# Attention and a gated unit in one fp32 kernel: a low part placed behind two maxima, the tails of the matmul units paired elsewhere, and the output weights split one round sooner

## The chip, the cores and the metric

The kernel runs on one core of a Trainium2 chip. The metric is the device time of the program in microseconds, as the median of several runs; lower is better. TensorE (PE) does the matmuls and its weight loads are listed apart (PEld); VectorE is DVE, ScalarE is ACT, GpSimd is POOL, and SyncE (SP) only issues transfers.

## The reference

`x` is 2048 x 448. One branch is a multi-head attention (16 heads of 28), the other a gated unit with 1792 hidden features; a gate computed from `x` mixes them.

```python
qkv = (x @ wqkv) -> q, k, v per head
scores = einsum("bhqd,bhkd->bhqk", q, k) * (Dh ** -0.5)
p = softmax(scores)
a = (p @ v, heads side by side) @ wo
gate = x @ W_gate
up = x @ W_up
gate = gate * (gate > 0)
b = (gate * up) @ W_down
g = sigmoid((x * gate_w).sum(-1, keepdims=True))
out = g * a + (1 - g) * b
```

## The kernel before

**Arithmetic.** Most matmuls run on float32 operands that are split into a rounded high part and a low part, the remainder. The high part is a cast (`act_high` on ACT, `dve_high` on DVE); the low part is a subtraction (`low` on DVE, `pool_low` on POOL). A product is then the sum of high x high, low x high and high x low. The contraction has 448 rows, three chunks of 128 and one of 64, and the 64 rows' high and low parts share one chunk, so one result tile of 128 x 512 takes `NT` = 11 passes (`TERMS`). Such a result is called a unit here. The last pass of a unit, its tail, needs 64 rows only.

**Order.** The order on every engine is the program's order, written out by hand; a tile pool only decides which buffer a tile gets and so what it has to wait for. PSUM has three tags: `s` with two tiles of 128 x 512, `mx` with two tiles of twice that size (`ps_w`), and `x` with two tiles of 128 x 512.

**First stage.** `qk` and `vproj` compute the projections, with matmuls for the first row maxima mixed in. `qk` ends with a cast on ACT, a `low` on DVE and a transfer from POOL's queue to `qk_d`. Before all that, `WARM` matmuls on zeros run on PE while the first inputs load. The last projection unit, `qk(0, 6)`, keeps its result in the second half of a tile named `pair`; the first half of that tile holds the raw weights of the first gate/up unit. `pair` sits in a buffer of the tag `Q`, and `load_q(2)` takes that tag's next buffer that comes free.

**Rounds.** The attention then runs in rounds (line 569). Each has an order string, read letter by letter: `s` is a score matmul of 128 x 512 with its exponential on ACT, `m` a maximum (two matmuls into a `ps_w` tile, one reduction on DVE), `x` one pass of a gate/up unit, `u` the split of the second half of the first gate/up weights with loads, `h` the paired tails. In a pair, the tail of one unit uses rows 0 to 63 of the array and that of the other rows 64 to 127; `SECOND` says which unit has the upper rows. At a round's end the weights of the next units are split (`split_f`) and `pv` multiplies the round's probabilities with V, 64 matmuls into a tile `po` that is copied to (ACT) or added to (DVE) the tile `os`.

There are 32 rounds: one `FIRST`, 28 `LONG` or `WIDE` ones, and three `LATE` ones, in which no maxima are left. A `LATE` round takes two score matmuls at a time into one `ps_w` tile, with one exponential over 128 x 1024 (`scores_pair`); its four gate/up units use the tag `s`, its `po` the tag `x`, and its relu and the casts of the weights run on DVE. The gate/up passes of the first unit follow `HIGH_FIRST`: six passes with the high weights, then those with the low ones.

**Last stage.** Five gate/up units of two results each (`gate_up`) are interleaved with the down projection (`down_mm`, 12 matmuls into `acc` each), then come the output projection (`wout`, with the weights `WO`) and more of the down projection. `split_wo` makes `WO` from the raw `wor` with two casts on ACT and two subtractions on POOL.

Lines that the steps touch: `WARM` line 34, `FIRST` 43, `LATE` 48, the end of `qk` 305 to 308, `SECOND` 430, `pv` 488, the loop over the rounds 569 to 630, `gate_up` 666.

Of the kernel before, what the change touches and what calls it, by code (L numbers as in the profile page):

```python
# [18 lines left out]
P = 128  # L19
# [7 lines left out]
NF = F // P  # L27
NB = 4
TB = 512
NK = S // P  # L30
SCALE = DH ** -0.5
VC = D + 2
NQ = 2 * D // P
WARM = 9

EARLY = (5, 5, 4, 4, 4, 3, 3, 3, 2, 2, 2, 2, 1, 1, 1, 1)

# [2 lines left out]

FIRST = "s" * 12 + "mmssmxxsxxusxmxsxsmxsmxsxsmxsxsmxsxsmxsxsxmsxsxmsxsxmsx"

LONG = "mxsmsxxxxxsmsxsmsxxsmsxsmsxxsmxxsmsxsxxsmsxxsxsmxsxsmsxxsmsxsmsxxsmsxsxxsmsmxssh"
WIDE = "sxxmxmxxsxxmsxxsxsmxxssxmxmxsxxsxxsxsmsxxsmxssxxxsmsxxsxmsxmsxsxmsxsmxsxsxxsmsxxsmsmsxxsxsh"

LATE = "ssxxxssxxxssxxxssxx" * 2 + "ssxxxssxxxssxxssxx" * 2 + "h"

ROUNDS = [(FIRST, 2)] + ([(LONG, 3)] * 2 + [(WIDE, 4)]) * 2 + [(LONG, 3)] * 2  # L50

# [6 lines left out]
NT = len(TERMS)  # L58
# [9 lines left out]
def gated_mix_kernel(ctx, tc, x, wq, wo, wgu, wd, out):  # L68
    nc = tc.nc
# [7 lines left out]
    def f32(ap):  # L77
        return ap.bitcast(F32)
# [4 lines left out]
    def ps_w(name):  # L83
        return psum.tile([P, 2, TB], F32, tag="mx", bufs=2, name=name)

    def ps_x(name):
        return psum.tile([P, TB], F32, tag="x", bufs=2, name=name)
# [7 lines left out]
    def low(dst, src, high):  # L95
        nc.vector.tensor_tensor(dst, src, f32(high), op=OP.subtract)  # L96
# [5 lines left out]
    qk_d = dram.tile([2, 2 * D, S], F32, name="qk_d")  # L102
# [92 lines left out]
    def xf(tb, b):  # L195
        return X[tb][b // 4][:, b % 4]

    WR, WS, HK, pair = {}, {}, {}, []

    def fetch_f(i):  # L200

# [8 lines left out]
    with tc.tile_pool(name="qkv", bufs=1) as pa:  # L210
# [89 lines left out]
        def qk(tb, c, terms=TERMS, among=()):  # L300
            ps = ps_any(f"qk_{tb}_{c}", c == NQ - 1)
            for n, (a, b) in enumerate(terms):
                nc.tensor.matmul(ps, W[:, a, c * P:(c + 1) * P], xf(tb, b), start=(n == 0), stop=(n == NT - 1))  # L303
                mix(n, among)
            st = st_tile(tb, c)
            act_high(st[:, 0], ps)
            low(st[:, 1], ps, st[:, 0])
            nc.gpsimd.dma_start(qk_d[:, c * P:(c + 1) * P, tb * TB:(tb + 1) * TB].rearrange("r d t -> d r t"), f32(st))

        def vproj(tb, t, among=()):  # L310
            ps = ps_any(f"v_{tb}_{t}", tb == 0 and t > 1)
# [26 lines left out]
        ps = ps_x("warm_ps")  # L338
        for n in range(WARM):
            nc.tensor.matmul(ps, warm[:, :P], warm, start=True, stop=True)  # L340
# [38 lines left out]
        units = [(qk, 3, 1), (qk, 2, 2), (qk, 3, 2)]  # L379
# [3 lines left out]
        units = units[2:]  # L383
        while units or vs:
            mixed += units[:1] + vs[:1]
            units, vs = units[1:], vs[1:]
        spills = {15 + 3 * k: (NB - 1 - k // 2, k % 2) for k in range(6)}
        m, first, ahead = 0, 9, 2 * LEAD + 4
        for n, (f, *a) in enumerate(mixed):
# [15 lines left out]
            among, ends = [], m  # L405
# [21 lines left out]
    att = stk.enter_context(tc.tile_pool(name="att", bufs=1))  # L427

    done = sum(n for _, n in ROUNDS) // 2
    SECOND = {sum(n for _, n in ROUNDS[:r + 1]) - 1 for r in range(len(ROUNDS)) if "h" in ROUNDS[r][0]}  # L430
    SECOND |= set(range(2 * done + 1, 2 * NB * NF, 2))

    def lane(k):
        return slice(64 * k, 64 * k + 64)
# [1 line left out]
    def split_f(i, high, low, part=(0, 1)):  # L436

        if part[0] == 0:
            WS[i] = fe.tile([P, 2, 7, P], F32R, name=f"wg_{i}", tag="wg", bufs=2)
        w, wr = WS[i], WR[i]  # L440
        for s in part:
            high(w[:, s, 0:3], wr[:, s, 0:3])
            low(w[:, s, 3:6], wr[:, s, 0:3], w[:, s, 0:3])
        if part[-1] == 1:
            high(w[:, :, 6], wr[:, :, 3])
            for s in range(2):
                rows = lane(1 - (2 * i + s in SECOND))
                low(w[rows, s, 6], wr[rows, s, 3], w[rows, s, 6])
            del WR[i]
# [4 lines left out]
    def gu_mm(ps, i, s, n):  # L454

        a, b = (BY_CHUNK if i else HIGH_FIRST)[n]
        rows = slice(0, P)
        if n == NT - 1 and 2 * i + s in SECOND | {k - 1 for k in SECOND}:
            rows = lane(int(2 * i + s in SECOND))
        nc.tensor.matmul(ps, WS[i][rows, s, a], xf(i // NF, b)[rows], start=(n == 0), stop=(n == NT - 1))  # L460
        c = b % 4
        if i % NF == NF - 1 and s and i < NB * NF - 1 and (n == NT - 1 or BY_CHUNK[n + 1][1] % 4 != c):
            for r in range(2):
                nc.sync.dma_start(f32(X[0][r])[:, c], x_d[i // NF + 1, r][:, c])
# [3 lines left out]
    def relu(i, ps, late=False):  # L468
        RL[i] = fe.tile([P, TB], F32, name=f"rl_{i}", tag="rl", bufs=2)
        if late:  # L470
            nc.vector.tensor_scalar_max(RL[i], ps, 0.0)
        else:
            nc.scalar.activation(RL[i], ps, AF.Relu)
# [4 lines left out]
    def spill_h(i, ps):  # L478
        h = fe.tile([P, TB], F32, name=f"h_{i}", tag="h", bufs=2)
        hidden(i, ps, h)  # L480
        h_d[i] = dram.tile([P, TB], F32, name=f"h_d_{i}")
        nc.gpsimd.dma_start(h_d[i], h)  # L482


    NI = H * NK
    OS, LS = {}, {}

    def pv(i0, ni, late):

        h = i0 // NK  # L490
        po = ps_x(f"po_{i0}") if late else ps_w(f"po_{i0}")[:, 0]
        for i in range(i0, i0 + ni):
            p = PT.pop(i)
            for j in range(NB):
                nc.tensor.matmul(po[32 * j:32 * j + 32], V[:, h // 4 % 2, i % NK, h % 4], p[:, j], start=(i == i0),  # L495
                                 stop=(i == i0 + ni - 1))
        if i0 % NK == 0:
            OS[h] = fe.tile([P, TB], F32, name=f"os_{h}", tag="os", bufs=2)
            nc.scalar.activation(OS[h], po, AF.Copy)
        else:  # L500
            nc.vector.tensor_tensor(OS[h], po, OS[h], op=OP.add)  # L501
        if (i0 + ni) % NK == 0:
            LS[h] = fe.tile([P, 16], F32, name=f"ls_{h}", tag="ls", bufs=2)
            nc.gpsimd.dma_start(LS[h], OS[h][DH::32].rearrange("j (p c) -> j p c", c=16))
# [39 lines left out]
    nxt = parts = i0 = 0  # L544
# [24 lines left out]
    for r, (order, nu) in enumerate(ROUNDS):  # L569
        ni = order.count("s") // NB  # L570
        late = order == LATE
        todo = list(range(nxt, nxt + nu))
        nxt += nu
        small_things(i0 // 4)
        if m % (2 * NK) == 0 and i0 <= NI - LEAD:
            smax_end(m // (2 * NK) - 1)
        if late and wor is None:
            wor = load_wo()

        passes = [(*divmod(k, 2), n) for k in todo for n in range(NT - ("h" in order and k >= nxt - 2))]  # L580
        units = []
        ns = 0
        for o in order:
            if o == "x" and not passes:
                continue
            if o == "s":
                i, j = i0 + 1 + ns // NB, ns % NB
                if ns == 4 * NB:
                    small_things(i0 // 4 + 1)
                if len(EARLY) <= i * NB + j < NI * NB and not late:  # L590
                    scores(i, j)
                elif late and i < NI and j % 2 == 0:
                    scores_pair(i, j)
                ns += 1
            elif o == "m":
                smax(m)
                m += 1
            elif o == "x":
                i, half, n = passes.pop(0)
                if n == 0:  # L600
                    ps = (ps_s if late else ps_x)(f"gu_{i}_{half}")
                    units.append((i, half, ps))
                gu_mm(units[-1][2], i, half, n)
                if n == NT - 1:
                    i, half, ps = units.pop()
                    spill_h(i, ps) if half else relu(i, ps, late)
            elif o == "u":
                split_f(0, act_high, pool_low, (1,))
                load_k(2)
                load_q(2)  # L610
                fetch_f(2)
                parts = 2
            elif o == "h":
                for i, half, ps in units:
                    gu_mm(ps, i, half, NT - 1)
                for i, half, ps in units:
                    spill_h(i, ps) if half else relu(i, ps, late)
        assert not passes, (r, passes)

        ready = nxt + (ROUNDS[r + 1][1] if r + 1 < len(ROUNDS) else 2)  # L620
        ready += ready % 2
        while parts < ready:
            split_f(parts // 2, dve_high if late else act_high, pool_low, (parts % 2,))
            parts += 1
            if parts % 2 == 0:
                fetch_f(parts // 2 + 1)
        pv(i0, ni, late)
        i0 += ni
        if late and i0 == NI:
            split_wo(wor)  # L630
    assert i0 == NI and m == len(maxima), (i0, m)
    stk.close()
# [33 lines left out]
    def gate_up(i):  # L666
        if i + 1 < NB * NF:
            split_f(i + 1, act_high, low)
        if i + 3 < NB * NF:
            fetch_f(i + 3)  # L670
        ps = ps_w(f"gu_{i}")
        for s in range(2):
            for n in range(NT - 1):
                gu_mm(ps[:, s], i, s, n)
        for s in range(2):
            gu_mm(ps[:, s], i, s, NT - 1)
        relu(i, ps[:, 0])
        spill_h(i, ps[:, 1])

# [51 lines left out]
    todo = [(gate_up, done), (row_sums, H - 1), (gate_up, done + 1)]  # L731
# [12 lines left out]
    for tb, load, split, at in ((0, 2, (3, 4), (5, 6, 7, 8)), (1, 5, (7, 9), (10, 11, 14, 14)), (2, 21, (23, 25), (28,) * 4),  # L744
                                (3, 35, (37, 39), (42,) * 4)):
        before(load, (fetch_o, tb))
        for k, i in enumerate(split):
            n = todo.index((down, i))
# [53 lines left out]
```

## Time and profile before

| | us |
|---|---|
| median of 3 runs | 1298.44 (1298.35, 1298.44, 1300.04) |
| the profiled execution, its time | 1299.74 |
| its span, first to last instruction | 1297.6 |
| outside the span | 2.14 |
| PE busy | 1290.2 |
| DVE busy | 817.3 |
| ACT busy | 763.0 |
| POOL busy | 367.3 |

The first `LATE` round begins at about 1018 us of the span, the last stage at 1092.3 us. A row of a timeline gives the start, how long the group lasted, the engine, the line, the operation, the tiles it writes and reads, the number of instructions merged, and in brackets the idle time before them with what ended it. Matmuls are pipelined: the time from one start to the next is the cost of a pass, and the duration shown for one is longer than that.

### The profile page before, as it was taken

How to read it: one execution, taken by the hardware profiler on the slowest of the kernel's cores; microseconds unless marked ns; L12 is line 12 of the kernel's file. 1: busy time of each engine (PE TensorE's matmuls, PEld its weight loads, DVE VectorE, ACT ScalarE, POOL GpSimd, SP SyncE). 2: the span in 40 equal slices, each digit the busy share in tenths (PEclk: the TensorE clock that was granted, in tenths of full speed). 3: DMA queues.
4: the chain of work that ended last, by engine and by line, in shares of the span. 5: the costliest groups of instructions: out<-in, count | busy, mean ns of one | idle time of the engine just before them, and what ended most of it. 6: DMA issues, size and time to landing. Idle time of an engine off the chain costs nothing.

```text
span 1297.6 us, 17707 instructions
## 1 busy us (share of the span) xinstructions
PE 1290.2 (99%) x6685; PEld 901.8 (69%) x6685; DVE 817.3 (63%) x849; ACT 763.0 (59%) x1387; POOL 367.3 (28%) x551
## 2 busy tenths in 40 slices
PE   9999999999999999999999999999999999999998
PEld 6888766666666666666666666666666656899997
DVE  6487766667677676777666667767677333663342
ACT  5212776666767777777776666767676755322121
POOL 3222122332313222222223322313132354641020
PEclk9999999999999999999999999999999999999999
DMA  9845523151427223141535142422341222744432
GB/s 311 293 159 230 154 75 98 57 122 47 118 66 192 73 78 99 54 100 47 135 104 121 57 104 69 110 68 82 78 135 35 92 82 88 247 136 151 135 109 77
DMA packets 53565, 148.87 MB, mean 115 GB/s; under 512 B 10024, under 2 KB 17128, under 8 KB 48872
## 3 DMA queue, kind: packets, MB, share of 16 engines
q1 hardware_dynamic: 36120, 98.34, 28.3%
q0 software_dynamic: 16928, 48.93, 10.4%
q8 instruction: 53, 0.87, 0.3%
q10 hardware_dynamic: 432, 0.46, 0.1%
q14 instruction: 32, 0.26, 0.1%
HBM read 102.06 MB, written 46.02 MB: 114 GB/s over the span
## 4 chain that ended last, share of the span: by engine, by line
PE 99%; DMA 0%; ACT 0%; DVE 0%; issue 0%; ACTq 0%
PE gu L460 22%; PE sm L152 19%; PE po L495 17%; PE s L178 17%; PE acc L703 11%; PE qk L303 6%; PE v L313 3%; PE wo L657 3%; PE s L189 2%; DMA wr<-wq 0%; PE mt L162 0%; DVE mx L154 0%; DVE pair L96 0%; DVE y L709 0%; ACT pair L90 0%
## 5 line engine op out<-in xcount | busy, mean ns | idle before, releaser
L154 DVE TENSOR_REDUCE mx<-sm 128x1 f32<-128x1024 f32 x512 | 614.2, 1221 | 107.5 <-PE sm L152 107.3
L180 ACT ACTIVATE P<-s 128x512 f32<-128x512 f32 x724 | 414.8, 598 | 164.0 <-PE s L178 124.0
L460 PE MATMUL gu<-X,wg 128*128 128x512 f32 (+1 forms) x1232 | 392.3, 402 | 0.0
L178 PE MATMUL s<-Q,K 114*128 114x512 f32 x932 | 368.7, 401 | 0.0
L152 PE MATMUL sm<-K,Q 112*128 112x512 f32 x1024 | 324.0, 398 | 1.6 <-DVE mx L154 1.6
L460 PEld LDWEIGHTS gu<-X,wg 128*128 128x128 f32 (+1 forms) x1232 | 226.4, 189 | 55.3 <-issue 10.7
L178 PEld LDWEIGHTS s<-Q,K 114*128 114x128 f32 x932 | 175.2, 188 | 89.0 <-ACT P L180 47.7
L152 PEld LDWEIGHTS sm<-K,Q 112*128 112x128 f32 x1024 | 192.2, 190 | 46.9 <-issue 10.1
L495 PE MATMUL po<-P,V 128*32 128x512 f32 x1600 | 181.0, 594 | 0.0
L482 POOL DMA_DIRECT2D h_d<-h x56 | 31.6, 563 | 524.9 <-DVE h L476 441.0
L99 POOL TENSOR_TENSOR wg<-wgr,wg 128x384 fp32r<-128x384 f32 x204 | 146.8, 737 | 8.1
L180 ACT ACTIVATE V<-s 128x512 f32<-128x512 f32 x208 | 119.6, 598 | 42.0 <-PE s L178 30.4
L703 PE MATMUL acc<-WD,hh 128*128 128x448 f32 x672 | 141.1, 368 | 0.0
L703 PEld LDWEIGHTS acc<-WD,hh 128*128 128x128 f32 x672 | 125.8, 188 | 13.3 <-ACT wg L90 0.5
L495 PEld LDWEIGHTS po<-P,V 128*32 128x32 f32 x1600 | 49.5, 110 | 111.2 <-issue 110.5
L90 ACT ACTIVATE hh<-hr 128x512 fp32r<-128x512 f32 x56 | 35.4, 632 | 124.8 <-PE acc L703 119.4
L96 DVE TENSOR_TENSOR hh<-hr,hh 128x512 fp32r<-128x512 f32 x56 | 46.6, 832 | 65.7 <-ACT hh L90 65.7
L303 PE MATMUL qk<-X,W 128*128 128x512 f32 x308 | 79.7, 402 | 0.6 <-ACT X L90 0.5
L303 PEld LDWEIGHTS qk<-X,W 128*128 128x128 f32 x308 | 59.0, 193 | 15.6 <-ACT X L90 1.4
L501 DVE TENSOR_TENSOR os<-po,os 128x512 f32<-128x512 f32 x16 | 11.1, 691 | 86.2 <-PE po L495 81.3
L96 DVE TENSOR_TENSOR mh<-mr,mh 16x128 fp32r<-16x128 f32 x16 | 6.0, 375 | 90.8 <-ACT mh L166 90.8
L90 ACT ACTIVATE wg<-wgr 128x384 fp32r<-128x384 f32 x150 | 60.3, 491 | 2.4 <-DMA wgr<-wgu 2.4
(74 smaller groups left out, 767.1 us busy)
## 6 DMA issues: line engine op xcount, KB each, us to landing
wgr<-wgu SPq DMA_DIRECT2D x55, 512.0 KB
K<-qk_d SPq DMA_DIRECT2D x64, 224.0 KB
Q<-qk_d SPq DMA_DIRECT2D x64, 224.0 KB
h_d<-h POOLq DMA_DIRECT2D x56, 256.0 KB, 2.3
hr<-h_d SPq DMA_DIRECT2D x56, 256.0 KB
qk_d<-st POOLq DMA_DIRECT2D x21, 512.0 KB, 3.6
x_d<-X POOLq DMA_DIRECT2D x6, 1024.0 KB, 5.2
X<-x_d SPq DMA_DIRECT2D x24, 256.0 KB
```

The costliest lines, as they stand in the source:

```text
L90: nc.scalar.activation(dst, src, AF.Copy)
L96: nc.vector.tensor_tensor(dst, src, f32(high), op=OP.subtract)
L99: nc.gpsimd.tensor_tensor(dst, src, f32(high), op=OP.subtract)
L152: nc.tensor.matmul(ps[:, c, :], Q[h][:GD, u * P:(u + 1) * P], K[h % 3][:GD, k0:k0 + TB], start=True, stop=True)
L154: nc.vector.tensor_reduce(MX[h][:, 2 * u + half:2 * u + half + 1], ps, axis=AX.XY, op=OP.max)
L178: nc.tensor.matmul(ps, K[h % 3][:GD + 2, kt * P:(kt + 1) * P], Q[h][:GD + 2, j * TB:(j + 1) * TB], start=True, stop=True)
L180: nc.scalar.activation(PT[i][:, j], ps, AF.Exp, scale=SCALE)
L303: nc.tensor.matmul(ps, W[:, a, c * P:(c + 1) * P], xf(tb, b), start=(n == 0), stop=(n == NT - 1))
L313: nc.tensor.matmul(ps[:, :VC], xf(tb, b)[:, t * P:(t + 1) * P], W[:, a, 2 * D:], start=(n == 0), stop=(n == NT - 1))
L460: nc.tensor.matmul(ps, WS[i][rows, s, a], xf(i // NF, b)[rows], start=(n == 0), stop=(n == NT - 1))
L495: nc.tensor.matmul(po[32 * j:32 * j + 32], V[:, h // 4 % 2, i % NK, h % 4], p[:, j], start=(i == i0), stop=(i == i0 + ni - 1))
L703: nc.tensor.matmul(ACC[i // NF][t][:, :D], HH[i][:, a, t * P:(t + 1) * P], WD[:, f, b], start=(f == 0 and n == 0), stop=(f == NF - 1 and n ...
```

## The change

1. `WARM` goes from 9 to 11.
2. The `low` of `qk(0, 6)` and its transfer are kept back in a list `sends`. A new letter `l` in `FIRST` runs them: behind the first two `m` of the round. On DVE the subtraction so stands behind two reductions instead of ahead of them. Behind `l` and two scores three passes `x` come before the third `m`, and `u` stands one pass later.
3. In a `LATE` round all four units keep back their tails, and two `h` at the end do two pairs. The first two units of a round use the tag `s`, the other two the tag `x`, and `po` moves to a `ps_w` tile (one half of it).
4. The five units of the last stage run their tails unpaired, over all 128 rows, so `SECOND` has only the units of the rounds. In all there are 34 pairs instead of 36.
5. In `LATE` rounds the casts of the gate/up weights run on ACT instead of DVE.
6. `split_wo` runs behind the second `LATE` round's `pv` instead of behind the third's.

```diff
-WARM = 9
+WARM = 11
-FIRST = "s" * 12 + "mmssmxxsxxusxmxsxsmxsmxsxsmxsxsmxsxsmxsxsxmsxsxmsxsxmsx"
+FIRST = "s" * 12 + "mmlssxxxmsxsxuxmsxmsxsxmsxsxmsxsxmsxsxmsxsxmsxsxmsxsxmsx"
-LATE = "ssxxxssxxxssxxxssxx" * 2 + "ssxxxssxxxssxxssxx" * 2 + "h"
+LATE = "ssxxxssxxxssxxssxx" * 4 + "hh"
...
             act_high(st[:, 0], ps)
-            low(st[:, 1], ps, st[:, 0])
-            nc.gpsimd.dma_start(qk_d[:, c * P:(c + 1) * P, tb * TB:(tb + 1) * TB].rearrange("r d t -> d r t"), f32(st))
+            def send():
+                low(st[:, 1], ps, st[:, 0])
+                nc.gpsimd.dma_start(qk_d[:, c * P:(c + 1) * P, tb * TB:(tb + 1) * TB].rearrange("r d t -> d r t"),
+                                    f32(st))
+            sends.append(send)
+            if (tb, c) != (0, NQ - 1):
+                sends.pop()()
...
-    SECOND = {sum(n for _, n in ROUNDS[:r + 1]) - 1 for r in range(len(ROUNDS)) if "h" in ROUNDS[r][0]}
-    SECOND |= set(range(2 * done + 1, 2 * NB * NF, 2))
+    SECOND = {sum(n for _, n in ROUNDS[:r + 1]) - 1 - 2 * k for r in range(len(ROUNDS))
+              for k in range(ROUNDS[r][0].count("h"))}
...
-        po = ps_x(f"po_{i0}") if late else ps_w(f"po_{i0}")[:, 0]
+        po = ps_w(f"po_{i0}")[:, 0]
...
-        passes = [(*divmod(k, 2), n) for k in todo for n in range(NT - ("h" in order and k >= nxt - 2))]
+        passes = [(*divmod(k, 2), n) for k in todo for n in range(NT - (k >= nxt - 2 * order.count("h")))]
...
-                    ps = (ps_s if late else ps_x)(f"gu_{i}_{half}")
+                    ps = (ps_s if late and len(units) < 2 else ps_x)(f"gu_{i}_{half}")
...
+            elif o == "l":
+                sends.pop()()
...
             elif o == "h":
-                for i, half, ps in units:
+                ends, units = units[:2], units[2:]
+                for i, half, ps in ends:
                     gu_mm(ps, i, half, NT - 1)
-                for i, half, ps in units:
+                for i, half, ps in ends:
                     spill_h(i, ps) if half else relu(i, ps, late)
...
-            split_f(parts // 2, dve_high if late else act_high, pool_low, (parts % 2,))
+            split_f(parts // 2, act_high, pool_low, (parts % 2,))
...
-        if late and i0 == NI:
+        if late and i0 == NI - NK // 2:
             split_wo(wor)
...
         for s in range(2):
-            for n in range(NT - 1):
+            for n in range(NT):
                 gu_mm(ps[:, s], i, s, n)
-        for s in range(2):
-            gu_mm(ps[:, s], i, s, NT - 1)
```

In the changed program ACT's queue behind the second `LATE` round reads: the round's last exponentials, six casts of weights, the copy of `po` to `os`, the two casts for `WO`, then the exponentials of the third `LATE` round. POOL's queue has the first subtraction for the first gate/up unit ahead of the transfer of `pair` instead of behind it.

More of the change, by code (lines that the diff above doesn't have):

```diff
@@ L196, in xf @@
         return X[tb][b // 4][:, b % 4]
-    WR, WS, HK, pair = {}, {}, {}, []
+    WR, WS, HK, pair, sends = {}, {}, {}, [], []
     def fetch_f(i):
@@ L486, in gated_mix_kernel, with pv @@
     OS, LS = {}, {}
-    def pv(i0, ni, late):
+    def pv(i0, ni):
         h = i0 // NK
-        po = ps_x(f"po_{i0}") if late else ps_w(f"po_{i0}")[:, 0]
+        po = ps_w(f"po_{i0}")[:, 0]
         for i in range(i0, i0 + ni):
@@ L626, in gated_mix_kernel @@
                 fetch_f(parts // 2 + 1)
-        pv(i0, ni, late)
+        pv(i0, ni)
         i0 += ni
-        if late and i0 == NI:
+        if late and i0 == NI - NK // 2:
             split_wo(wor)
```

## The prediction

> **What bounds the kernel now.** I read the page's head and the chain that ended last, then timelines of the places that the diff touches.
>
> ```profile
> span 1297.6 us, 17707 instructions
> ...
> PE 99%; DMA 0%; ACT 0%; DVE 0%; issue 0%; ACTq 0%
> PE gu L460 22%; PE sm L152 19%; PE po L495 17%; PE s L178 17%; PE acc L703 11%; PE qk L303 6%; PE v L313 3%; PE wo L657 3%; PE s L189 2%; DMA wr<-wq 0%; PE mt L162 0%; DVE mx L154 0%; DVE pair L96 0%; DVE y L709 0%; ACT pair L90 0%
> ```
>
> The chain is PE nearly throughout, so time comes only from fewer passes, cheaper switches between kinds of pass, or PE stalls. The chain names one stall outside the start: `DVE mx`, `DVE pair`, `ACT pair`.
>
> **Part 1, the low part behind two maxima.**
>
> ```profile
> 143.74 1.09 PE L152 MATMUL sm<-K,Q 112*128 112x512 f32 x4
> 144.44 0.60 ACT L90 ACTIVATE pair<-qk 128x512 fp32r<-128x512 f32 x1
> 144.67 0.64 PE L178 MATMUL s<-Q,K 114*128 114x512 f32 x2
> 144.91 0.53 ACT L90 ACTIVATE wg<-pair 128x384 fp32r<-128x384 f32 x1
> 145.07 0.69 DVE L96 TENSOR_TENSOR pair<-qk,pair 128x512 fp32r<-128x512 f32 x1 [1.79 <-ACT pair L90]
> 145.32 1.09 ACT L180 ACTIVATE P<-s 128x512 f32<-128x512 f32 x2
> 145.68 3.47 DVE L154 TENSOR_REDUCE mx<-sm 128x1 f32<-128x1024 f32 x3
> 146.05 0.72 POOL L308 DMA_DIRECT2D qk_d<-pair  x1 [4.14 <-DVE pair L96]
> 146.94 0.73 PE L152 MATMUL sm<-K,Q 112*128 112x512 f32 x2 [1.64 <-DVE mx L154]
> ```
>
> DVE stood idle 1.79 us for ACT's cast of `pair`, with the first maximum ready behind it. The third `m` needs that maximum's PSUM tile. PE could have gone on at 144.67 + 2 x 0.234 = 145.14 (0.234 is a pass, see the next fence) and went on at 146.94: 1.80 lost, and 0.10 for a weight load that nothing covers (0.73 for the two after the wait, against 0.64 for the two scores): 1.90.
>
> After the change DVE can begin the first maximum when its matmuls end, at about 144.4, and be done by about 145.65 (a third of 3.47 is 1.16). What is late next is the first `x`: its high weights come from ACT's cast that ends at 144.91 + 0.53 = 145.44, a place that the edit leaves as it is. So PE waits from 145.14 to about 145.5, 0.36, plus again 0.10. The third `m` follows three passes later, about 146.3, when its tile is free. `HIGH_FIRST` keeps POOL's subtraction out of the first six passes. The subtraction (0.69) moves behind two reductions, where DVE has the three passes' time. Gain 1.90 - 0.46 = 1.44. Bounds: 1.90 if the cast is early enough; 0.35 if it comes behind the two exponentials (1.09) after it.
>
> The held transfer of `pair` moves too, about 1.4 us later on POOL's queue; its follower is the rival below.
>
> **Parts 2 and 3, the tails.** A pass, a switch and a pair:
>
> ```profile
> 160.89 0.40 PE L460 MATMUL gu<-X,wg 128*128 128x512 f32 x1
> 161.22 4.50 PE L495 MATMUL po<-P,V 128*32 128x512 f32 x40
> ...
> 527.60 0.65 PE L178 MATMUL s<-Q,K 114*128 114x512 f32 x2
> 528.17 0.49 PE L460 MATMUL gu<-X,wg 64*128 64x512 f32 x2
> 528.60 0.64 PE L495 MATMUL po<-V 128*32 128x512 f32 x4
> ...
> 1068.22 0.74 PE L189 MATMUL s<-Q,K 114*128 114x512 f32 x2
> 1068.80 0.86 PE L460 MATMUL gu<-X,wg 128*128 128x512 f32 x3
> 1069.50 0.63 PE L189 MATMUL s<-Q,K 114*128 114x512 f32 x2
> 1070.66 0.63 PE L189 MATMUL s<-Q,K 114*128 114x512 f32 x2
> ```
>
> Three passes take 1069.50 - 1068.80 = 0.70, so 0.234 each. Without a pair the switch to `po` makes the last pass 161.22 - 160.89 = 0.33, 0.10 more. With a pair: the two passes before it take 528.17 - 527.60 = 0.57, 0.10 over two passes, and the pair itself 0.43. So a lone pair before `po` costs 0.53 against 0.234 + 0.33 = 0.56 for two plain tails: it hardly pays.
>
> In a `LATE` round a second pair replaces two plain passes (0.47) and enters and leaves the split array no more often. Its cost lies between one pass (0.234), if its weights load while the first pair runs, and 0.43, if each pair stands alone. I take 0.234:
>
> ```profile
> 1036.31 7.00 PE po L495 x64
> ...
> L495 PE MATMUL po<-P,V 128*32 128x512 f32 x1600 | 181.0, 594 | 0.0
> L460 PEld LDWEIGHTS gu<-X,wg 128*128 128x128 f32 (+1 forms) x1232 | 226.4, 189 | 55.3 <-issue 10.7
> ```
>
> `po` also runs in a split array, 16 groups of four in 7.00, 0.44 a group, and each matmul shows 0.59: groups overlap by 0.15, as plain passes do (0.40 shown, 0.234 spent). The lone pair shows 0.49 for 0.43. So a following group in one mode is pipelined. Gain 3 x (0.47 - 0.234) = 0.70; bounds 0.12 and 0.75.
>
> The loads of plain passes (189 ns) are hidden under passes on the same rows. The Trainium skill speaks against that for split arrays: "TensorE: Matmul & The Clock Gate", Part 3, under what overlaps, says a weight load overlaps a running matmul only where the row groups differ. By that rule the second pair, on the rows of the first, costs 0.43 and the gain is 0.12; the row of `gu` loads disagrees for the whole array, and no run here shows two pairs in a row.
>
> `po` in a `ps_w` tile: the second `scores_pair` after it (1069.50) needs that tile copied. The copy ends at 1068.96 (row below), so no wait; without that half microsecond it would cost what the copy is late.
>
> **Part 4, no pairs in the last stage.**
>
> ```profile
> 1105.42 5.27 PE L460 MATMUL gu<-X,wg 128*128 128x512 f32 x22
> 1110.62 2.70 PE L703 MATMUL acc<-WD,hh 128*128 128x448 f32 x12
> ...
> 1133.32 2.63 PE L703 MATMUL acc<-WD,hh 128*128 128x448 f32 x12
> ```
>
> A unit with a pair takes 1110.62 - 1105.42 = 5.20; 22 plain passes are 22 x 0.234 = 5.15. The 12 `acc` matmuls behind a pair show 2.70, those behind `wo`, with no switch, 2.63. So 0.05 + 0.07 = 0.12 each, five times: 0.60. Bounds 0.25 (only the unit) and 0.80 (0.10 for entry and exit each, less the pair's saving of about 0.04).
>
> **Parts 5 and 6, ACT's queue.**
>
> ```profile
> 1068.36 0.60 ACT L499 ACTIVATE os<-po 128x512 f32<-128x512 f32 x1 [6.85 <-PE po L495]
> 1069.06 2.19 ACT L191 ACTIVATE V<-s 128x1024 f32<-128x1024 f32 x2
> ...
> 1084.22 1.78 ACT L90 ACTIVATE WO<-wor 128x1344 fp32r<-128x1344 f32 x2
> 1085.90 1.23 ACT L90 ACTIVATE wg<-wgr 128x384 fp32r<-128x384 f32 x3
> ...
> L191 ACT ACTIVATE V<-s x8: 1024/1027/1027, 1032.2 to 1070.2; 128x1024 f32<-128x1024 f32 x8
> ```
>
> The casts of weights (2 x 1.23) fall into ACT's 6.85 us of idle time under `po`: nothing. The two `WO` casts (1.78) are another matter: they now stand behind the copy of `po` (ends 1068.96) and ahead of the third `LATE` round's exponentials. ACT's neighbours overlap by about 0.1, as the rows of part 1 show (144.91 starts before 144.44 + 0.60), so the first exponential starts at about 1070.55 instead of 1069.06 and ends 1.03 later, at 1071.6. The third `scores_pair` reuses its tile; it was due at 1070.66. PE stalls 0.95, plus 0.10 for the uncovered load: a loss of 1.05. It was free before: at 1084.22 no exponential followed. Bounds: 0 if PE has slack that I don't see, 1.4 if ACT, which then runs without pause, makes the next pairs late as well.
>
> **`WARM`.**
>
> ```profile
> 5.71 7.53 PE L303 MATMUL qk<-X,W 128*128 128x512 f32 x23 [0.49 <-ACT X L90]
> ...
> 1.20:5.20 4.00, 4.00 (x9) 1.18 (x9) 0.03 (x1) 1.73 (x3) 3.88 (x4) 1.00 0.82 262
> ...
> 5.70:9.70 4.00, 3.99 (x9) 3.10 (x10) 3.92 (x8) 3.40 (x9) 1.16 (x6) 1.00 1.01 343
> 9.70:13.00 3.30, 3.30 (x15) 2.51 (x14) 2.87 (x6) 2.98 (x6) 0.89 (x1) 1.00 0.79 272
> ...
> 10.42 0.76 PEld L303 LDWEIGHTS qk<-X,W 128*128 128x128 f32 x4 [0.28 <-DVE W L96]
> ```
>
> PE runs at half rate until about 9.7 (9 passes in 4.0, then 15 in 3.3). Two more warm matmuls of 0.44 (nine in 4.0) fill the gap of 0.49 before the first pass and may delay it by up to 2 x 0.44 - 0.49 = 0.4. Either way PE meets DVE's weights at 10.42, for which it already waited 0.28 in loading: 0. Bounds: a loss of 0.4; a gain of 1.9 in executions that have nine slow passes behind that point (9 x (0.44 - 0.234)).
>
> **Sum.** -1.44 - 0.70 - 0.60 + 1.05 + 0 = -1.69. The profiled execution was 1297.6 + 2.14 = 1299.74, so it would be 1298.05. It stands 1.30 above the median of the runs, and the terms do not depend on that: 1298.44 - 1.69 = 1296.75, called 1296.7. Terms at their ends: -1.90 - 0.75 - 0.80 + 0 - 1.9 = -5.35, and -0.35 - 0.12 - 0.25 + 1.4 + 0.4 = +1.1.
>
> **The rivals.**
>
> *The `WO` casts cost nothing.* For: ACT has 6.85 idle just before. Against: they stand behind the copy of `po`, which waits for PE. Sum -2.74: 1295.7.
>
> *The rate comes earlier.* If the gap before 5.71 kept PE at half rate until 9.7, closing it speeds up as many as the nine passes up to 9.7: 1.9 less, 1294.8. Against: the wait for DVE at 10.42, by which PE would only wait longer; for: other executions may reach full rate later than this one. The Trainium skill has this rule ("TensorE: Matmul & The Clock Gate", Part 1): a free-running window of about 3.4 us has to be busy, and a gap spoils it. The half rate after a gap agrees; the wait at 10.42 speaks against the gain.
>
> *Tails and first passes gain little.* The second pair costs 0.43 (gain 0.12 instead of 0.70) and the first `x` waits for a later cast: about -0.5 to -1.1: 1297.5.
>
> *The held transfer makes head 2 late.*
>
> ```profile
> qk_d<-pair POOLq DMA_DIRECT2D x1, 512.0 KB, 7.9
> ...
> L139 SPq DMA_DIRECT2D Q<-qk_d x4: 306/377/383, 154.2 to 155.4; - x4
> ...
> 168.26 0.71 PE L152 MATMUL sm<-K,Q 112*128 112x512 f32 x2
> ```
>
> `pair` is released when its transfer lands, 146.05 + 7.9 = 153.95, and the loads of `Q` for head 2 went out at 154.2. They would go out 1.4 later and PE reach head 2 (168.26) 1.5 sooner, so 12.9 us between issue and use become 10. From the point where the loads take over 10 us, each one more costs PE one; at 16 us the sum is 6 - 1.7 = +4.3: 1302.7. Against: the transfer of 512 KB took 7.9, these are 224 KB each.
>
> **How the numbers follow.** Forecast 0.49; `WO` free 0.16; rate 0.14; little gain 0.16; head 2 late 0.05. 0.2% is 2.6 us, about what a measurement of this kernel can tell from no change. Faster by more needs 1295.8: `WO` free (0.11 of its 0.16), rate (0.12) and the lower edge of the forecast (0.10): 0.33. Slower: head 2, 0.05. The rest, 0.62, is within. The range 1294.7 to 1298.2 takes in all rivals but the last and cuts both tails; all but one case have one sign.
>
> **What would show it.** Right: PE's wait for `DVE mx` near 145 gone, one of 0.4 for `ACT wg` in its place; 0.66 for two pairs together before `po`; `acc` groups that show 2.63; an ACT row `WO` near 1067 and a PE wait of 1 for an exponential behind it. Wrong: no such wait, full rate before 9 us with the second unit earlier than 10.4, or a PE wait for `Q` near 167.

## The result and the profile after

| | before | after |
|---|---|---|
| median, us | 1298.41 (11 runs, 1297.92 to 1300.25) | 1296.11 (11 runs, 1295.85 to 1296.35) |
| profiled execution: time, span, outside the span | 1299.74, 1297.6, 2.14 | 1295.85, 1294.1, 1.75 |

The medians differ by 2.30 us, 0.18%; the ratio over all runs is 0.9979, 0.21%, 95% interval 0.997 to 0.9988. So the gain is clear of zero and lies at the edge of the 0.2% that the prediction calls no change. The time lies in the range given (1294.7 to 1298.2) and 0.6 under the forecast.

One thing is plain from the two rows of runs: the kernel before scatters over 2.3 us, the changed one over 0.5. That scatter turns out to be part of the answer.

The head and the chain of the page after (columns as before): the entry `DVE mx`, `DVE pair`, `ACT pair` of the stall is gone, and `ACT WO` is new.

```profile
span 1294.1 us, 17710 instructions
...
PE 98%; ACT 0%; DMA 0%; SPq 0%; DVE 0%; issue 0%; ACTq 0%
PE gu L468 22%; PE sm L152 19%; PE po L503 17%; PE s L178 17%; PE acc L712 11%; PE qk L303 5%; PE v L321 3%; PE wo L668 3%; PE s L189 2%; DMA wr<-wq 0%; PE mt L162 0%; ACT WO L90 0%; SPq L253 0%; DVE W L96 0%; ACT V L191 0%
```

The timeline after, at the place of the stall:

```profile
143.94 2.35 DVE L154 TENSOR_REDUCE mx<-sm 128x1 f32<-128x1024 f32 x2 [1.13 <-PE sm L152]
143.96 0.60 ACT L90 ACTIVATE pair<-qk 128x512 fp32r<-128x512 f32 x1
144.19 0.63 PE L178 MATMUL s<-Q,K 114*128 114x512 f32 x2
144.44 0.53 ACT L90 ACTIVATE wg<-pair 128x384 fp32r<-128x384 f32 x1
145.02 0.97 PE L468 MATMUL gu<-X,wg 128*128 128x512 f32 x3 [0.20 <-ACT wg L90]
145.83 0.64 PE L152 MATMUL sm<-K,Q 112*128 112x512 f32 x2
146.21 0.68 DVE L96 TENSOR_TENSOR pair<-qk,pair 128x512 fp32r<-128x512 f32 x1
```

DVE now begins the first maximum at 143.94, under ACT's cast of `pair`, and does the subtraction at 146.21. PE could go on at 144.19 + 2 x 0.234 = 144.66 and went on at 145.02, 0.36 later, released by ACT's cast for `wg`. The three passes take 0.81 until 145.83, against 0.70: the uncovered load, 0.1. It is the step of the prediction to the hundredth.

The PE timeline at the end of the first `LATE` round:

```profile
1031.50 1.06 PE L468 MATMUL gu<-X,wg 128*128 128x512 f32 x5
1032.49 0.64 PE L503 MATMUL po<-P,V 128*32 128x512 f32 x4
```

The five are one plain pass and two pairs: 0.99 from the first row's start to `po`. The plain pass with its switch is 0.33 (the 0.234 and 0.10 of the prediction), so two pairs take 0.66 and the second 0.66 - 0.43 = 0.23.

The timeline behind the second `LATE` round:

```profile
1064.46 0.60 ACT L507 ACTIVATE os<-po 128x512 f32<-128x512 f32 x1 [4.72 <-PE po L503]
1064.95 1.78 ACT L90 ACTIVATE WO<-wor 128x1344 fp32r<-128x1344 f32 x2
1066.63 1.93 ACT L191 ACTIVATE V<-s 128x1024 f32<-128x1024 f32 x2
1067.70 0.72 PE L189 MATMUL s<-Q,K 114*128 114x512 f32 x2 [0.78 <-ACT V L191]
```

The two casts for `WO` stand between the copy of `po` and the exponentials, and PE waits for the first exponential. The pass before it began at 1066.53 (three passes of 0.23 from 1066.06), so 1.17 instead of 0.234 went by: 0.94 lost, plus 0.10 for the load (0.72 shown for the two scores, 0.63 elsewhere).

The PE timeline of the last stage:

```profile
1102.11 5.31 PE L468 MATMUL gu<-X,wg 128*128 128x512 f32 x22
1107.27 2.64 PE L712 MATMUL acc<-WD,hh 128*128 128x448 f32 x12
```

A unit takes 1107.27 - 1102.11 = 5.16 (5.20 before), and `acc` shows 2.64 (2.70 before): 0.04 + 0.06 a unit, some 0.5 for five.

And the start, from the view of windows after and the timeline of weight loads after. A row of windows gives the stretch, its length, the busy time of PE with the number of its matmuls, the same of PEld, DVE, ACT and POOL, then the granted clock (the share of its full rate that PE was given), the DMA share and GB/s.

```profile
5.50:9.50 4.00, 3.89 (x14) 2.67 (x12) 3.92 (x9) 3.42 (x10) 1.34 (x7) 1.00 1.06 378
```

```profile
5.44 3.16 PEld L303 LDWEIGHTS qk<-X,W 128*128 128x128 f32 x10 [0.28 <-ACT X L90]
10.03 3.31 PEld L303 LDWEIGHTS qk<-X,W 128*128 128x128 f32 x15 [0.40 <-DVE W L96]
```

The 14 are 12 passes of the projection and the last two warm matmuls; before, nine passes fell into these four microseconds. In the trace after, the passes start 0.43 apart up to 7.15 and 0.23 to 0.25 apart from there to 8.57, so the full rate does come before 9 us. (The clock's first record in a trace is its rise to full rate, here at 7.18, so the 1.00 in this row says nothing of the time before it.) The load that waits for DVE's weights is at 10.03; it was at 10.42.

### The profile page after: what moved, and what is told of

Same layout as the page of the kernel before. It is cut to its first block, busy times and chain, and to the rows that moved or that the text cites. A ratio compares the mean times of both kernels' runs of the same rounds, so it can differ in the third digit from the quotient of the medians.

```text
span 1294.1 us, 17710 instructions
## 1 busy us (share of the span) xinstructions
PE 1287.5 (99%) x6687; PEld 901.8 (70%) x6687; DVE 806.1 (62%) x834; ACT 767.0 (59%) x1402; POOL 365.8 (28%) x551
## 4 chain that ended last, share of the span: by engine, by line
PE 98%; ACT 0%; DMA 0%; SPq 0%; DVE 0%; issue 0%; ACTq 0%
PE gu L468 22%; PE sm L152 19%; PE po L503 17%; PE s L178 17%; PE acc L712 11%; PE qk L303 5%; PE v L321 3%; PE wo L668 3%; PE s L189 2%; DMA wr<-wq 0%; PE mt L162 0%; ACT WO L90 0%; SPq L253 0%; DVE W L96 0%; ACT V L191 0%
## 5 line engine op out<-in xcount | busy, mean ns | idle before, releaser
L90 ACT ACTIVATE wg<-wgr 128x384 fp32r<-128x384 f32 x165 | 66.3, 491 | 2.3 <-PE gu L468 1.2
```

The source lines that it names most:

```text
L90: nc.scalar.activation(dst, src, AF.Copy)
```

## The experiments

Twelve kernels ran, four on each of three chips, each set beside the kernel before. The kernel before had medians of 1298.99 (33 runs), 1300.68 (20) and 1299.28 (27) there, so times are compared within a set.

### One part alone

First set: the kernel before with one part of the change.

```diff
-WARM = 9
+WARM = 11
```

> The kernel before with 11 warm matmuls instead of 9, nothing else. Theory of the sum (places): in the profile after the change the first unit reached full rate at about 7.2 us instead of 9.7 and the second unit's low weights came 0.40 us sooner, so 0.4 us less: about 1298.0 where the kernel before gives 1298.4, and every projection matmul behind 11 us is 0.4 us earlier. Rival (rate): in the changed kernel's profile the passes of the LONG rounds are shorter throughout (the lead over the profile of before grows from 1.98 us at the first po to 3.49 at the 29th); if the closed gap at the start does that, this run alone gains about 1.9 us (0.4 + 1.5) and the rounds take 29.97 instead of 30.03 us.

Measured 1299.60 (1298.22 to 1300.24), ratio 1.0004, interval 0.9995 to 1.0013. The windows and the weight loads of this kernel:

```profile
5.50:9.50 4.00, 3.83 (x13) 1.00 1.04 364
```

```profile
10.19 3.11 PEld L303 LDWEIGHTS qk<-X,W 128*128 128x128 f32 x14 [0.40 <-DVE W L96]
```

The row is of PE alone. The rate is up early here too (13 matmuls, two of them warm), PE then waits for DVE's weights, and the time has not moved. `WARM` is worth nothing that these runs can tell.

Part 1, with the changed `FIRST`, `sends` and the letter `l`:

```diff
-FIRST = "s" * 12 + "mmssmxxsxxusxmxsxsmx...
+FIRST = "s" * 12 + "mmlssxxxmsxsxuxmsxms...
```

> The kernel before with the held low part, the letter l and the new FIRST, nothing else. Theory of the sum: the stall of 1.80 + 0.10 us at 145 goes, one of 0.36 + 0.10 for ACT's cast of the weights comes, 1.44 us less: about 1297.0 where the kernel before gives 1298.4. Rival (late transfer): the transfer of pair and with it the loads of Q for head 2 are 1.4 us later and PE waits at the first maximum of head 2 (about 167 us); then less than 1 us is left of the gain.

Measured 1296.77 (1296.48 to 1297.53), ratio 0.9986, interval 0.9977 to 0.9995: 2.2 under the median before. The PE timeline of this kernel has the same wait for ACT's `wg`:

```profile
144.52 0.63 PE L178 MATMUL s<-Q,K 114*128 114x512 f32 x2
145.35 0.97 PE L468 MATMUL gu<-X,wg 128*128 128x512 f32 x3 [0.20 <-ACT wg L90]
146.16 0.64 PE L152 MATMUL sm<-K,Q 112*128 112x512 f32 x2
```

The first `po` starts 1.63 sooner than in the profile of before, and 0.09 of that comes from data that arrived sooner at 10 us (10.33 against 10.42), so PE gains 1.54. The median moved by 0.7 more than the trace accounts for.

The last stage unpaired:

```diff
-    SECOND |= set(range(2 * done + 1, 2 * NB * NF, 2))
...
-            for n in range(NT - 1):
+            for n in range(NT):
```

> The kernel before with the tails of the last stage's five units unpaired, nothing else. Theory of the sum: 0.12 us a unit, 0.60 us less: about 1297.8 where the kernel before gives 1298.4; acc groups behind these units show 2.63 instead of 2.70. Rival (a pair saves a pass): five more passes of 0.234, 1.2 us more: 1299.6.

Measured 1298.15 (1297.83 to 1300.16), ratio 0.9995, interval 0.9986 to 1.0004. In the trace a unit with its `acc` group takes 7.63, 0.11 less than the 7.74 of before. That is the size expected; the medians (0.84 apart) and their interval, which holds no change, do not show it.

The `LATE` rounds with two pairs and the casts on ACT:

```diff
-LATE = "ssxxxssxxxssxxxssxx" * 2 + "ssxxxssxxxssxxssxx" * 2 + "h"
+LATE = "ssxxxssxxxssxxssxx" * 4 + "hh"
```

> The kernel before with the LATE rounds of the change (two pairs of tails each, po in a ps_w tile, casts of weights on ACT), but with the output weights split behind the third LATE round as before, the pairs in the last stage kept, 9 warm matmuls and the old FIRST. Theory of the sum: the second pair costs 0.34 us with its entry and exit unchanged and replaces 0.47, so 0.23 us a round, 0.70 us less: about 1297.7 where the kernel before gives 1298.4, and 0.66 us from the first of the two pairs to po. Rival (ACT sets the pace): with two passes fewer to cover 16 exponentials a round, scores wait for ACT, and the gain is under 0.3 us.

Measured 1297.51 (1296.98 to 1299.15), ratio 0.9991, interval 0.9983 to 1.0: 1.48 under the median before, where 0.70 was expected. In the trace the three rounds take 0.56 less. Two things stand in the rest. The time outside the span of the profiled execution is 1298.88 - 1297.1 = 1.78, as in the changed kernel; the other three of this set have about 2.1. Some 0.35 of the gain of the `LATE` rounds lies outside the span, and nothing in the trace says what it is. The two levels hold for every execution whose span is on record: 1.72 to 1.90 with the new `LATE` rounds, 2.06 to 2.24 without. And this execution shows something that the run was not made for. Windows of the kernel with the `LATE` rounds alone:

```profile
140.00:144.00 4.00, 4.00 (x19) 3.16 (x18) 2.45 (x2) 2.32 (x6) 1.11 (x2) 1.00 0.33 131
147.90:151.40 3.50, 3.50 (x10) 2.70 (x9) 1.77 (x2) 1.91 (x5) 1.87 (x3) 0.53 0.94 173
151.40:154.90 3.50, 3.50 (x16) 2.84 (x16) 3.34 (x7) 2.75 (x5) 0.00 (x0) 0.99 0.49 150
```

The same window of the kernel with only the last stage changed, which has the same stall ahead of it:

```profile
147.90:151.40 3.50, 3.50 (x16) 2.70 (x15) 2.80 (x5) 2.79 (x7) 1.75 (x4) 1.00 0.83 173
```

Just behind the stall PE ran for 3.5 us at a granted clock of 0.53, with 10 passes where the other had 16. Six passes of 0.234 are 1.4 us. The stall that part 1 removes so has a second price, paid in some executions only. It would explain why the runs of the kernels with the stall lie in two groups about 1.5 apart, why the changed kernel has one, and the 0.7 above.

The mean granted clock on record for every run bears this out. Half rate for 3.4 of 1298 us makes it 0.9987, so a run given as 1.000 had no such stretch. Of these runs alone, the kernel before has a median of 1298.41 (20 runs), the one with part 1 1296.77 (nine) and the one with the `LATE` rounds 1297.39 (six): 1.64 and 1.02 less, near the 1.54 and the 0.56 + 0.35 that the traces account for. Of all runs with their clock on record, these and those below, 20 of 124 with the stall stand at 0.998, and none of 80 without it or with it filled. A smaller scatter has another cause: three of the 11 runs with part 1 alone lie some 0.8 above the middle of the rest, all at 1.000.

### Where the wait for `WO` comes from, and whether the stall makes the two groups

Second set. The split of `WO` put back behind the third `LATE` round:

```diff
-        if late and i0 == NI - NK // 2:
+        if late and i0 == NI:
```

> The changed kernel with the split of the output weights back behind the third LATE round. Theory (the two WO casts, ahead of the third LATE round's exponentials in ACT's queue, hold PE for 0.94 + 0.10, and nothing in the last stage needs them that early): the PE wait near 1067 is gone, no new one comes in the last stage, 1296.11 - 1.04 = 1295.1. Rival (ACT, which in the changed kernel also casts the gate/up weights of the LATE rounds, reaches the WO casts so late that the output projection or the last stage's relus wait for it): a PE wait of about 1 behind 1090 instead, 1296.1 or more.

The same round as in the change, but ahead of `pv`, so ahead of the copy of `po` on ACT:

```diff
+        if late and i0 + ni == NI - NK // 2:
+            split_wo(wor)
         pv(i0, ni)
         i0 += ni
-        if late and i0 == NI - NK // 2:
-            split_wo(wor)
```

> The changed kernel with the split of the output weights in the same (second) LATE round, but issued ahead of the copy of po instead of behind it. Theory (what costs is the place in ACT's queue: ahead of po's copy the casts, 1.78, fall into ACT's idle 6.85 under po): the PE wait near 1067 is gone, 1296.11 - 1.04 = 1295.1, as with the split put back. Rival (a round sooner costs as such, since ACT is full from there on or POOL's subtractions come in the way of the next weights): the wait stays or turns into one for the copy of po or for a weight: 1296.1.

The old `FIRST`, with the subtraction not held (the stall is back):

> The changed kernel with the old order FIRST and the subtraction of the last projection unit not held, so with the stall of 2.05 near 145 again. Theory (the stall costs 1.54 more than its successor, and in a part of the executions PE runs a stretch of some 3.4 us at half rate behind it, about 1.5 more): most executions near 1296.11 + 1.54 = 1297.65, and 2 to 5 of 11 some 1.0 to 2 above them, at a mean granted clock of 0.998 or 0.999. Rival (the two groups of executions have nothing to do with the stall: it is chance, or the LATE rounds or the last stage): one group as in the changed kernel, highest less lowest under 0.6, all at about 1297.6.

The changed kernel again:

> The changed kernel once more, beside the other three on the same chip. Theory (without the stall no execution falls back to half rate): 1296.1, highest less lowest under 0.6, while the kernel before shows two groups, 1298.0 to 1298.9 and 1299.0 to 1301. Rival (the grouping depends on chip or session): executions 1.0 to 2 above the lowest here too.

| | median | runs | span of the profile |
|---|---|---|---|
| `WO` put back | 1297.18 | 5, 1295.43 to 1297.52 | 1293.7 |
| `WO` ahead of the copy | 1296.42 | 5, 1294.86 to 1297.01 | 1293.0 |
| old `FIRST` | 1300.53 | 11, 1299.04 to 1301.02 | 1297.6 |
| changed kernel | 1297.83 | 10, 1297.52 to 1298.33 | 1296.2 |

*The stall.* With the old `FIRST` four runs lie from 1299.04 to 1299.84 and seven from 1300.44 to 1301.02; without the stall, on the same chip, all ten lie within 0.81. The lowest runs differ by 1.52, the medians by 2.70. So the grouping goes with the stall, and the upper group is larger (seven of 11) than expected (two to five). Both rows of runs lie 1.4 or more above what was expected; most of that is the pass, below.

*`WO`.* With the split put back the wait near 1067 is gone, yet the span is only 0.4 under the 1294.1 of the changed kernel's first profile (an execution with the same pass), not 1.04. The timeline of this kernel shows why (POOL, SP's queue and PE):

```profile
1090.19 4.34 POOL L99 TENSOR_TENSOR WO<-wor,WO 128x1344 fp32r<-128x1344 f32 x2
...
1094.57 0.33 SPq L695 DMA_DIRECT2D wdr<-wd  x1
1094.94 0.42 SPq L697 DMA_DIRECT2D hr<-h_d  x1
...
1098.63 3.24 PE L712 MATMUL acc<-WD,hh 128*128 128x448 f32 x12
```

POOL's two subtractions for `WO` end at 1090.19 + 4.34 = 1094.53, and at 1094.57 the loads for the last stage go out: their tiles lie in the pool that opens when that of `wor` is closed. The first `acc` group so takes 3.24 instead of 2.63, waiting for `hh` and `WD`. With the split ahead of the copy of `po`, in the earlier round:

```profile
1059.60 1.77 ACT L90 ACTIVATE WO<-wor 128x1344 fp32r<-128x1344 f32 x2
1064.42 0.60 ACT L507 ACTIVATE os<-po 128x512 f32<-128x512 f32 x1 [3.04 <-PE po L503]
...
1088.28 0.33 SPq L695 DMA_DIRECT2D wdr<-wd  x1
1088.66 0.42 SPq L697 DMA_DIRECT2D hr<-h_d  x1
...
1098.56 2.63 PE L712 MATMUL acc<-WD,hh 128*128 128x448 f32 x12
```

The casts lie in ACT's idle time under `po`, the loads leave at 1088.28, and `acc` takes 2.63. This span is 1.1 under that of the changed kernel: the whole wait back, the early loads kept. In the set's medians it is 1.41 under, a difference that rests on five runs and also holds what follows.

*The pass.* The changed kernel itself is 1.72 slower in this set than in the first session (1297.83 against 1296.11), and its lowest run here lies above its highest there. The view of windows over the same 800 us, of the changed kernel in its first profile and, in the second fence, in this set:

```profile
200.00:1000.00 800.00, 800.00 (x4293) 1.00 0.35 90
```

```profile
200.00:1000.00 800.00, 800.00 (x4288) 1.00 0.36 90
```

Five of 4293 passes fewer at a granted clock of 1.00: passes are longer, but not all. Start by start, the second execution lags the first by 0.72 at 40 us, 0.74 at 160, 2.15 at 1000 and 2.12 at 1280. So 1.4 us arise in the rounds, and none in the projections or in the last stage. Within the rounds the `po` groups take 7.00 in both, so it is the score, maximum and gate/up passes that are longer, by some 0.5 ns of 234. The profiled execution of the kernel before has 4287 in this window, which fits its standing 1.30 above the median. It belongs to the execution, not to the kernel. What sets it stays open.

### Filling the stall, and what is left of it

Third set. The kernel before, with its stall, but matmuls on zeros in it (a new letter `f`):

```diff
-FIRST = "s" * 12 + "mmssmxx...
+FIRST = "s" * 12 + "mmssfmxx...
...
+            elif o == "f":
+                ps = ps_x("fill")
+                for n in range(7):
+                    nc.tensor.matmul(ps, warm[:, :P], warm, start=True, stop=True)
```

> The kernel before with seven matmuls on zeros, 0.22 each at full rate, put on PE between the two scores and the third maximum of the first round, where it stood idle for 1.8. Nothing else is changed, so the wait for the first maximum stays. Theory (the idle time of PE throws it back to half rate in a part of the executions, and this is what puts those 1 to 3 above the others): the time of the kernel before in its lower group, no execution more than 0.8 above the lowest, and a median 1 to 2 under that of the kernel before on this chip. Rival (the fall-back has another cause, such as the maxima or the chip): the same two groups and the same median as the kernel before, or up to 0.5 more for the matmuls.

Measured 1298.47 (11 runs). Ten lie from 1298.30 to 1298.60 and one at 1299.29, 0.99 above the lowest, where at most 0.8 was expected; of the 27 runs of the kernel before on this chip 11 lie from 1297.97 to 1298.87 and 16 from 1299.15 to 1300.29. The timeline of the kernel with the fill (it has records of six of the seven matmuls):

```profile
145.36 1.46 PE L610 MATMUL fill<-warm 128*128 128x512 bf16 x6
145.68 3.48 DVE L154 TENSOR_REDUCE mx<-sm 128x1 f32<-128x1024 f32 x3
...
146.94 0.73 PE L152 MATMUL sm<-K,Q 112*128 112x512 f32 x2
```

The third maximum starts at 146.94 as it did before: the wait for DVE is whole, only PE is not idle in it. Yet the upper group is gone, all but one run, and that one has a mean granted clock of 1.000, so its 1299.29 is not the half rate. So it is PE's idleness, not the wait, that brings the half rate. The median fell by 0.81, less than the 1 to 2 expected, and the ratio's interval (0.9987 to 1.0004) holds no change; what shows the mechanism is the scatter.

ACT's cast of `pair` held as well, so that the cast for `wg` goes first:

```diff
-            act_high(st[:, 0], ps)
             def send():
+                act_high(st[:, 0], ps)
                 low(st[:, 1], ps, st[:, 0])
```

> The changed kernel with ACT's cast of the last projection unit held as well, together with its subtraction, so that ACT's cast for the first gate/up weights stands ahead of it. Theory (the 0.36 that PE waits for that cast plus 0.10 for an uncovered weight load are all that is left of the stall): PE's wait for ACT wg near 145 is gone, 0.46 less than the changed kernel on the same chip. Rival (the next thing is as late: the third maximum, which then comes 0.4 sooner, finds its tile still being reduced, or the exponentials stand behind the cast): the wait moves by some 0.4 and the time stays.

Both that and the split of `WO` ahead of the copy:

> The changed kernel with both: the cast of the last projection unit held, and the split of the output weights ahead of the copy of po in the same round. Theory (both waits are apart from each other, 0.46 near 145 and 1.04 near 1067): 1.5 less than the changed kernel on the same chip. Rival (a gain in front is eaten by a later wait for data that comes by its own clock): 1.1 less or under.

The changed kernel as their reference:

> The changed kernel beside the other three on the same chip, as their reference. Expected 1296.1 if the chip gives the shorter pass (0.2330) and 1297.8 if it gives the longer one (0.2335), all executions within 0.8 of each other.

Measured: the cast 1296.34 (11 runs, 1296.15 to 1296.73), both 1295.18 (six runs, 1295.06 to 1295.37), the changed kernel 1296.56 (ten runs, 1295.96 to 1296.83). The timeline with the cast held, of PE and, for the maxima, of DVE:

```profile
145.04 0.86 PE L467 MATMUL gu<-X,wg 128*128 128x512 f32 x3
...
147.19 2.35 DVE L154 TENSOR_REDUCE mx<-sm 128x1 f32<-128x1024 f32 x2
...
148.07 0.40 PE L467 MATMUL gu<-X,wg 128*128 128x512 f32 x1
148.46 0.74 PE L152 MATMUL sm<-K,Q 112*128 112x512 f32 x2
...
151.12 0.39 PE L467 MATMUL gu<-X,wg 128*128 128x512 f32 x1
151.59 0.74 PE L152 MATMUL sm<-K,Q 112*128 112x512 f32 x2
```

The wait for `wg` at 145.04 is gone, and two maxima now come late: 0.39 and 0.47 from the pass before them instead of 0.234, each with a load of 0.1 behind it. That is 0.6 for the 0.46 saved. The first of the two starts at 148.46, as the first of DVE's two reductions from 147.19 ends (1.22 each, 148.41). The rival was right: behind PE stands DVE with its maxima, and PE gains nothing by reaching them sooner. The version with both edits is 1.38 under the changed kernel and beats both given kernels (ratio to before 0.9968, interval 0.9956 to 0.998). The cast adds nothing to that by its trace, and the `WO` edit alone had the shorter span (1293.0 against 1293.3, on different chips).

## Why the prediction was right, and where it was off

It forecast 1296.7, 1.69 less, and no change within 0.2%; it was 1296.11, 2.30 less, and at the edge of no change. The places of the gains and of the one loss were right, and so were their sizes to 0.15. That the call of no change survived is partly luck: three terms that the sum did not have, at the foot of the table, brought the time to that edge. The steps, against what the traces show (part 1 from the run with it alone):

| step | predicted | trace |
|---|---|---|
| part 1, stall for a shorter wait | -1.44 | -1.54 |
| second pairs, three rounds | -0.70 | -0.56 |
| last stage unpaired | -0.60 | -0.54 |
| `WO` casts ahead of exponentials | +1.05 | +1.04 |
| `WARM` | 0 | 0 |
| time outside the span | not seen | -0.35 |
| last stage's loads leave sooner | not seen | 0 against the profile of before, -0.16 to -0.74 against others |
| half rate behind the stall | not seen | -1.4 in some executions |

- *Part 1.* The wait for `DVE mx` is gone and one of 0.36 for ACT's `wg` in its place. But the prediction priced the stall by its length alone. It named half rate only for the start, as the rival "the rate comes earlier", and did not ask what 1.8 us of idle PE do to the rate later on. The profile of before could not show it: that execution went on at full rate.
- *The pairs.* The second pair costs 0.23, the size forecast, but not as one more pass: the trace has the pairs' starts at 1031.83 and 1032.17 and `po` at 1032.49. The second pair so comes 0.34 behind the first, and `po` 0.33 behind it, where it came 0.43 behind a lone pair. The 0.23 is the difference of the sums. The small shortfall is waits of 0.03 before a `scores_pair` whose tile an exponential still reads: three in each of the last two `LATE` rounds, where the old order had one in each.
- *The last stage.* Right, by rows.
- *`WO`.* The place, the releaser and the size were right. The step that failed is the sentence "It was free before": the casts were free, but the split also holds the memory of the last stage's tiles. The part was costed by its ACT casts only, not by POOL's subtractions behind them and by what waits for their tile. In the profile of before PE had no wait there. Of the other kernels with the split late, the one with `WARM` alone shows it best, in its PE timeline:

```profile
1101.57 3.05 PE L703 MATMUL acc<-WD,hh 128*128 128x448 f32 x12 [0.32 <-ACT hh L90]
```

- *`WARM`.* The text said that full rate before 9 us with the second unit earlier than 10.4 would show it wrong, and the profile after has both. That sign was badly chosen, for the early rate is not the work of the two matmuls. By the clock's records the rate rose at 9.71 in the profile of before and at 7.18 in that of the change, but at 4.72 to 5.54 in the four other kernels with nine warm matmuls (part 1 alone, the last stage alone, the `LATE` rounds alone, the fill). The run with `WARM` alone agrees: full rate at 5.24, the data at 10.19, the time unmoved. When DVE's weights come varies from execution to execution by more than this; the profile of the changed kernel in the third set has that load at 10.86.
- *The rivals.* "`WO` costs nothing" fell with the wait at 1067.70, "tails and first passes gain little" with the second pair's 0.23, "head 2 late" did not appear: nothing in the chain after waits for `Q`. "The rate comes earlier" was right about the rate and wrong about the time.
- *The base.* Making the sum against the median and not the profiled execution was right, for a reason not known then: that execution had the longer passes.

The span terms sum to -1.6, with the time outside to -1.95 and with the earlier loads to between -2.1 and -2.7. The medians moved by 2.30. In that session seven of 11 runs of the kernel before lay in its lower group, whose middle is 1298.3, so most of the half rate's price is not in the median; in the second and third set, where the upper group is the larger, the change is worth 2.85 (1300.68 to 1297.83) and 2.72 (1299.28 to 1296.56).

## What to carry to other kernels

A stall of the engine that bounds the kernel can cost more than its length, and one profiled execution may not show it: look at the scatter of the runs, and at each run's granted clock, before pricing a stall. A wait that can't be removed can be filled with matmuls that do nothing, which here took the upper group of runs away. When work is moved earlier in the program, ask besides its own queue what its buffer's end releases; here that was the loads of the whole next stage. And put work that an engine does for later ahead of an instruction that waits, not behind it: the same two casts cost 1.04 on one side of a copy and nothing on the other.

## What the runs showed of the hardware

*Half rate after a short stall.* In the one profile that caught it, of the `LATE` rounds alone, PE stood idle for 1.65 us until 146.64, and from 148.08 to 151.50, 3.41 us, its passes took 0.43 instead of 0.23 (granted clock 0.53 in the window shown). In that trace the clock rose to full rate 143.36 us before it fell, which is 42 times 3.413; the one stretch at full rate in the other traces is 377 or 378 times as long. So the changes lie on a grid of 3.41 us. The stretch of the grid just before the fall, 144.67 to 148.08, holds the whole idle time. In the other four profiles with the stall unfilled, none of which fell, a border of the grid lies in it (in the one of the last stage alone, at its very start). Five traces fit a dependence on where the idle time falls on the grid; they do not prove it. The length agrees with the Trainium skill ("TensorE: Matmul & The Clock Gate", Part 1, "What's actually happening"), which has a free-running window of about 3.4 us. By the same page of the Trainium skill half rate comes after at least one idle window of that length; here half of one was enough, and the measurement decides.

*Two pairs in a row.* In the Trainium skill (the same page, Part 3, under what overlaps) a weight load overlaps running matmuls only on other row groups. The weights of the second pair, on the same rows as the first, began to load 0.11 after the first pair's start and were loaded 0.04 before the second's, and two pairs cost 0.66 where a lone one costs 0.43. The load ran under the first pair, so that rule does not hold here.

*Two lengths of a pass.* 4293 or 4288 passes in 800 us for one and the same kernel at a granted clock of 1.00, 1.4 us over the rounds; the projections, the `po` groups and the last stage keep their times. Both lengths came up on the second chip within the set, the shorter in the profiles of the two `WO` kernels. The cause is open.
